# Attention and two MLPs on one core: scores on eight PE tiles, transposes of two tokens in the first two batches

## The chip, the cores and the metric

The kernel runs on one core of one Trainium2 chip. The time is the device time of one execution in microseconds (us). The core has a matrix engine (PE, with weight loads shown as PEld), a vector engine (DVE), a scalar engine (ACT), GpSimd (POOL, nearly unused here) and one queue, SP, from which this kernel issues all its transfers.

## The reference

There are 8 batches of 8 heads, 576 tokens and 64 elements a head, and 32 packed tokens `p` a head. Two attentions follow each other, and then two MLPs over all 4608 tokens (512 wide, 2048 hidden):

```python
s = scale * np.matmul(qq, kk.transpose(0, 1, 3, 2))      # sm_attn(qq, kk, vv)
a = np.exp(s - max(s)); a = a / (sum(a) + 1e-09); return np.matmul(a, vv)
...
p_packed = sm_attn(p, k, v)                # 32 x 576 scores a head
out = sm_attn(q, p_packed, p_packed)       # 576 x 32 scores a head
x = out.transpose(0, 2, 1, 3).reshape(B * S, H * D)
h = x @ w_in;  x = (h * sigmoid(h)) @ w_out
h = x @ w_in2; return (h * np.cos(h)) @ w_out2
```

## The kernel before

**Planner.** Every instruction is first recorded in a `Plan`, which then orders all engines at once: a list scheduler takes, on each engine, the ready operation that is due first, with a cost for each operation from a table (`price`) and a fixed cost for each transfer that SP issues. What stands in the code in one place can so stand elsewhere in the program. All transfers stand in one queue, SP, in the planned order: one that waits for a buffer holds those behind it.

**Stages.** The first MLP runs over four pairs of batches (`first`, with banks `hb` and `acc`); attention of the next batches runs between its matmuls. The second MLP follows (`second`) and holds no attention. In the first pair the MLP is cut into 16 runs, each of which ends with four writes of partial sums from two `ysb` buffers to DRAM (`ydram`, `ypart`).

**Attention.** `stage1(b, g)` and `stage2(b, g)` treat four heads, as `g` of 2 and two head pairs `j`; `h2` is the head in a pair. `turned` gives keys or queries with the 64 elements of a head on partitions and tokens in columns, two heads above each other (partitions 64*`h2`). For batches 0 and 1 (`Boot`), tokens come from `bx`, 96 rows of 6 tokens, and PE turns them by matmuls with the identity: 6 for a bank (`st`), 12 for a tile `bkt`, then a `copy` to SBUF on ACT or DVE, strided for queries. For batches 2 to 7 (`Steady`), four transfers fill a `kin` buffer in blocks of 32 x 32 and DVE transposes it into a `big` buffer.

**Scores.** `scores` writes two banks, one for each half `hf` of the tokens (288 columns). A bank takes four matmuls, one for each head of the four: 64 rows by 32 columns of the PE array, at row 64*`h2` and column 64*`j` + 32*`place(b, h2)`, where `place` is `(b + h2) % 2`. The four lie on four different tiles of the array; the second bank uses the same four tiles again. There are two calls for each batch and `g` (one in each stage), 32 in all: 24 in `Steady`, 8 in `Boot`. In stage 1 the stationary operand is `pbd`, filled by `place_p` (four transfers into `pin`, two DVE transposes for each batch); in stage 2 it is `ppf`, which holds each head on both partition halves.

**Products.** `products` multiplies `ppf` with the first MLP's weights on tiles of the same shape, with 512 columns: for batch 0 alone at the start (four tiles, one bank), later for two batches at once (`mb` and `sb`), whose `place` differs, so that the eight matmuls of a pass lie on eight tiles.

**Start.** Batches 0 and 1 stand before and within the first MLP steps. PE runs fillers there (`mb<-ident`), and the weights of the first MLP are decoded on ACT and DVE (tiles `wd`, `wde`, `wy`, `w1e`, `w`).

Of the kernel before, what the change touches and what calls it, by code (L numbers as in the profile page):

```python
# [12 lines left out]
F32 = mybir.dt.float32  # L13
# [66 lines left out]
class Plan:  # L80
# [4 lines left out]
    PE, DVE, ACT, POOL, DMA, NONE = "PE", "DVE", "ACT", "POOL", "DMA", "NONE"  # L85
# [72 lines left out]
    def price(self, engine, f, out, ins):  # L158

        n = math.prod(out.shape[1:])  # L160
        m = max([math.prod(x.shape[1:]) for x in ins], default=n)
        sbuf = all(not str(x.space).endswith("PSUM") for x in ins)
        strided = 44 if ins and n >= 96 and ins[0].ap[-1][0] == 2 else 110 if n >= 96 and out.ap[-1][0] > 2 else 0
        if engine == self.PE:
            if f == "transpose":
                return 3 + n / 1.2, 0

            if ins[0].dtype == F32R:
                return n / 2.4 + (18 if n == 512 else 13), 0
            rows, k = out.shape[0], ins[0].shape[0]  # L170
            if rows == 128:
                return n * 3.33 + 10, 0
            if rows == 64:
                return n * 0.82, 0
            return {64: 30 if k == 96 else 37, 288: 127, 512: 117}[n], 0
        if engine == self.DVE:
            if f == "transpose":
                return (67 if sbuf else 160) + n / 0.92, 0
            fast = sbuf and f in ("tensor_copy", "tensor_scalar", "memset") and m == n
            if f == "scalar_tensor_tensor" and sbuf and ins[0].dtype == F32:  # L180
                return 67 + n / 0.53, 0
            return 67 + max(max(m, n) / (1.92 if fast else 0.96), 60 if f == "reciprocal" else 0) + strided, 0
        if engine == self.ACT:
            return (94 if sbuf else 51) + max(m, n) / 1.2 + (190 if f == "accumulate" else 0) + (105 if f == "sin" else 0) + strided, 0
        if engine == self.POOL:
            return 149 + (1.7 if any(0 in [st for st, _ in x.ap] for x in ins) else 2.1) * n, 0
        run = min(map(self.contiguous, (out, *ins)))
        return self.ISSUE, 4 * math.prod(out.shape) / (260 if run >= 128 else 150)
# [217 lines left out]
def attention_mlps_kernel(  # L406
# [13 lines left out]
    B, H, S, D = q.shape  # L420
# [30 lines left out]
    def ring(ts):  # L451

        at = cycle(ts)
        return lambda: next(at)
# [16 lines left out]
    def tiles(pl, shape, dtype, name, n):  # L471

        ts = [pl.tile(shape, dtype, name=f"{name}{i}") for i in range(n)]
        cells.setdefault(pl, []).extend(t.tensor.name for t in ts)
        return ts


    def place(b, h2):
        return (b + h2) % 2
# [48 lines left out]
    def copy(dst, src):  # L528
        with plan.either():
            A.copy(dst, src)  # L530
            V.tensor_copy(dst, src)
# [81 lines left out]
        combine(v[1], v[1], v[2], ALU.subtract)  # L613
        put(y[1], 5)

    pins = ring(tiles(att, [P, H // 2, 32], F32, "pin", 1))
    maxes = ring(tiles(att, [P, 2], F32, "mx", 2))
    ms = ring(tiles(att, [P, 1], F32, "m", 2))
    sumss = ring(tiles(att, [P, 1], F32, "sums", 2))
# [4 lines left out]
    a2s = ring(tiles(a2p, [P, 2, S], F32R, "a2", 4))  # L624

    def place_p(b):
        t = pins()
        for h2 in range(2):
            for x in range(2):
                r = h2 * 64 + x * 32  # L630
                DMA.dma_start(t[r : r + 32], p[b, h2::2, :, 32 * x : 32 * x + 32].rearrange("j n d -> n j d"))
        for h2 in range(2):
            r, x = slice(64 * h2, 64 * h2 + 64), NP * place(b, h2)
            V.transpose(pbds[b % 2][r, :, x : x + NP], t[r].rearrange("p j d -> p (j d)"))

    def cut(t, shape):
        t = t[:, : math.prod(shape[1:])]
# [4 lines left out]

    class Steady:


        def __init__(self):
            self.kins = ring(tiles(att, [P, NB, 32], F32, "kin", 2))
# [6 lines left out]
        def turned(self, src, b, g, bank):  # L654

            ts = []
            for j in range(2):
                x = self.kins()
                for h2 in range(2):
                    for c in range(2):  # L660
                        r = h2 * 64 + c * 32
                        DMA.dma_start(
                            x[r : r + 32],
                            src[b, 4 * g + 2 * j + h2, :, 32 * c : 32 * c + 32].rearrange("(n r) d -> r n d", r=32),
                        )
                t = self.get("kt", [P, S], g, j)
                V.transpose(t, x.rearrange("p n d -> p (n d)"))
                ts.append(t)
            return ts
# [16 lines left out]

    class Boot:


        chunks = [slice(c, c + CH) for c in range(0, S, CH)]  # L690

# [21 lines left out]
        def turned(self, src, b, g, bank):  # L713
            x = self.x["k" if src is k else "q"]
            ts = []
            for j in range(2):
                t = self.get("kt", [P, S], g, j)
                hp = 2 * g + j
                for i in range(2):
                    st = bank()  # L720
                    with plan.together():
                        for c in range(3):
                            for h2 in range(2):
                                T.matmul(
                                    st[D * h2 : D * h2 + D, c * CH : (c + 1) * CH],
                                    x[:CH, 2 * hp + h2, 3 * i + c, :],
                                    ident[:CH, :CH],
                                    start=True,
                                    stop=True,
                                )  # L730
                    part = st[:, :HALF].rearrange("p (c r) -> p c r", c=3)
                    if src is k:
                        to = t.rearrange("p (c r) -> p c r", c=NCH)
                    else:
                        to = t.rearrange("p (r c) -> p c r", c=NCH)
                    copy(to[:, 3 * i : 3 * i + 3], part)
                ts.append(t)
            return ts

        def values(self, b, g):  # L740
            return lambda c, h2, j: self.x["v"][:CH, 4 * g + 2 * j + h2, c, :]

    ppf = {}
    a2 = {}

    def scores(b, keys, queries, bank):

        sts = [bank()[:, :HALF] for _ in range(2)]
        with plan.together():
            for hf, st in enumerate(sts):  # L750
                c = slice(hf * HALF, (hf + 1) * HALF)
                for j in range(2):
                    for h2 in range(2):
                        r, x = 64 * h2, 32 * place(b, h2)
                        T.matmul(
                            st[64 * j + x : 64 * j + x + 32],
                            keys[r : r + 64, j, x : x + 32],
                            queries[j][r : r + 64, c],
                            start=True,
                            stop=True,  # L760
                        )
        return sts

    def stage1(b, g, bank, mem):
# [2 lines left out]
        kt = mem.turned(k, b, g, bank)  # L767
        a1 = mem.get("a1", [P, S], g)
        mx = maxes()
        sts = scores(b, pbds[b % 2][:, 2 * g : 2 * g + 2], kt, bank)  # L770
        for hf, st in enumerate(sts):
            V.tensor_reduce(mx[:, hf : hf + 1], st, axis=AX.X, op=ALU.max)
            copy(a1[:, hf * HALF : (hf + 1) * HALF], st)
# [39 lines left out]
    def stage2(b, g, bank, mem):  # L813

        qt = mem.turned(q, b, g, bank)
        s = mem.get("s", [P, NB, 32], g)
        sf = s.rearrange("p n r -> p (n r)")
        for hf, st in enumerate(scores(b, ppf[b, g], qt, bank)):
            V.transpose(sf[:, hf * HALF : (hf + 1) * HALF], st)
        mx = mx2s()  # L820
        V.tensor_reduce(mx, s, axis=AX.X, op=ALU.max)
        combine(s, s, mx.unsqueeze(2).to_broadcast([P, NB, 32]), ALU.subtract)
        A.activation(sf, sf, AF.Exp, scale=SCALE)
        rs = rs2s()
        V.tensor_reduce(rs, s, axis=AX.X, op=ALU.add)
        V.tensor_scalar(rs, rs, 1e-9, None, op0=ALU.add)
        V.reciprocal(rs, rs)
        combine(s, s, rs.unsqueeze(2).to_broadcast([P, NB, 32]), ALU.mult)
        at = mem.get("at", [P, S], g)
        V.transpose(at, sf)  # L830
        d = a2s()
        split(d, at)
        a2[b, g] = d
# [190 lines left out]
    def output(i, t):  # L1024

        o = oring()
        if t % 2:
            V.tensor_scalar(o, acc[t], WEIGHT**-2, None, op0=ALU.mult)
        else:
            A.activation(o, acc[t], AF.Copy, scale=WEIGHT**-2)  # L1030
        p0 = order[i] * TB + t % 2 * P
        cuts = [p0] + list(range(p0 // HALF * HALF + HALF, p0 + P, HALF)) + [p0 + P]
        for a, b in zip(cuts, cuts[1:]):
            r0 = a // HALF * S + t // 2 * HALF + a % HALF
            DMA.dma_start(out[r0 : r0 + b - a, :], o[a - p0 : b - p0])

    gt, st, m5s = {}, {}, {}

# [223 lines left out]
```

## Time and profile before

| | |
|---|---|
| time, median of 3 runs | 1538.78 us (1537.59 to 1538.87) |
| the profiled execution | 1536.31 us, span 1534.6 us |
| PE busy | 1516.4 us (99%) |
| DVE busy | 1154.6 us (75%) |
| ACT busy | 786.0 us (51%) |
| mean granted TensorE clock | 0.998 of full speed |

Busy time of PE counts overlapped matmuls once, but its matmuls are pipelined: how long a block takes is read from the start of its first matmul to the start of the next block, not from the durations, which reach into the next block. A full-precision matmul here is two instructions in the trace, a transpose one.

### The profile page before, as it was taken

What the parts mean: (1) busy time and instruction counts of PE and PEld (TensorE: products, weight loads), DVE (VectorE), ACT (ScalarE), POOL (GpSimd) and SP (SyncE); (2) the same over time, 40 slices, a digit from 0 to 9 for tenths busy, and PEclk for the clock granted to TensorE, in tenths of its full rate; (3) what the DMA queues carried; (4) which work ended last, traced back from release to release, by engine and by line L of the source; (5) the groups of instructions that cost most, each with busy time, mean ns of one, the idle gap of its engine ahead of it and who ended that gap; (6) DMA issues with size and microseconds to landing.
All of it is one profiled execution on the core that took longest, in us unless ns stands there. A gap on an engine that the chain in (4) does not pass through costs nothing.

```text
span 1534.6 us, 31226 instructions
## 1 busy us (share of the span) xinstructions
PE 1516.4 (99%) x11640; PEld 1371.0 (89%) x11640; DVE 1154.6 (75%) x2413; ACT 786.0 (51%) x1678; POOL 0.7 (0%) x6
## 2 busy tenths in 40 slices
PE   9899999999999999999999999999999999999998
PEld 7689878999889998899999999999998999999997
DVE  5999567786888778784467777888878777777665
ACT  5886544555555555554354444544444445444443
POOL 0000000000000000000000000000000000000000
PEclk9999999999999999999999999999999999999999
DMA  9786474556864766541685757778665657575560
GB/s 239 230 245 194 113 158 127 170 130 167 188 205 144 183 148 190 186 156 51 209 267 177 231 175 246 245 228 252 214 214 191 214 177 230 174 230 178 184 195 35
DMA packets 304855, 287.29 MB, mean 187 GB/s; under 512 B 166464, under 2 KB 215104, under 8 KB 304704
## 3 DMA queue, kind: packets, MB, share of 16 engines
q1 hardware_dynamic: 304704, 285.30, 62.4%
q8 instruction: 92, 1.51, 0.4%
q14 instruction: 59, 0.48, 0.1%
HBM read 232.00 MB, written 53.22 MB: 186 GB/s over the span
## 4 chain that ended last, share of the span: by engine, by line
PE 90%; DMA 4%; DVE 3%; ACT 2%; issue 1%; SPq 0%; ACTq 0%; DVEq 0%
PE acc L208 50%; PE hb L208 22%; PE sb L208 9%; PE mb L208 9%; DMA bx<-in_v 1%; DVE r L208 1%; DMA kin<-in_k 0%; DMA ysb<-ypart 0%; DMA ypart<-ysb 0%; DMA w1dram<-w1e 0%; DMA wd<-in_moe_w_in 0%; ACT bkt L208 0%; SPq L208 0%; DVE w L208 0%; DVE g L208 0%
## 5 line engine op out<-in xcount | busy, mean ns | idle before, releaser
L208 PE MATMUL acc<-g,w 128*128 128x288 f32 x3072 | 472.0, 297 | 3.0 <-ACT ysb L208 1.8
L208 PEld LDWEIGHTS acc<-g,w 128*128 128x128 f32 x3072 | 425.4, 188 | 34.5 <-issue 24.3
L208 PE MATMUL acc<-w,g 128*128 128x512 f32 x1728 | 431.6, 392 | 0.0
L208 PEld LDWEIGHTS acc<-w,g 128*128 128x128 f32 x1728 | 310.9, 189 | 55.7
L208 PE MATMUL hb<-a,w 128*128 128x288 f32 x1536 | 262.3, 298 | 4.8 <-DVE a L208 2.2
L208 PEld LDWEIGHTS hb<-a,w 128*128 128x128 f32 x1536 | 221.7, 188 | 16.6 <-issue 8.7
L208 DVE TENSOR_TENSOR g<-gf,g 128x288 fp32r<-128x288 f32 x256 | 114.9, 453 | 73.0 <-PE acc L208 52.1
L208 ACT CAST g<-gf 128x288 fp32r<-128x288 f32 x238 | 102.9, 435 | 122.4 <-PE acc L208 100.7
L208 ACT ACTIVATE gf<-hb 128x288 f32<-128x288 f32 x256 | 103.5, 411 | 102.8 <-PE hb L208 88.0
L208 DVE SCALAR_TENSOR_TENSOR gf<-gf,hb 128x288 f32<-128x288 f32 x256 | 111.8, 449 | 48.3 <-ACT gf L208 46.7
L208 ACT ACTIVATE r<-r,half_pi 128x512 f32<-128x512 f32 x144 | 103.8, 722 | 35.7 <-DVE r L208 35.5
L208 ACT CAST g<-r 128x512 fp32r<-128x512 f32 x144 | 89.7, 623 | 59.3 <-DVE r L208 57.3
L208 PEld LDWEIGHTS hb<-w,w 128*128 128x128 f32 x729 | 103.8, 190 | 7.9
L208 PE MATMUL hb<-w,w 128*128 128x256 f32 x729 | 110.0, 282 | 0.0
L208 DVE TENSOR_TENSOR g<-r,g 128x512 fp32r<-128x512 f32 x144 | 98.9, 687 | 11.1 <-ACT g L208 10.7
L208 DVE SCALAR_TENSOR_TENSOR r<-n,r 128x512 f32<-128x512 int32 x144 | 99.0, 688 | 2.2
L208 ACT ACTIVATE n<-hb 128x512 int32<-128x512 f32 x72 | 43.1, 599 | 111.9 <-PE hb L208 105.6
L208 DVE TENSOR_TENSOR hb<-hb,gf 128x256 f32<-128x256 f32 x72 | 31.1, 432 | 69.9 <-PE hb L208 69.8
L208 ACT ACTIVATE n<-mb 128x512 int32<-128x512 f32 x36 | 21.5, 598 | 98.4 <-PE mb L208 98.4
L208 PE MATMUL mb<-w,w 128*128 128x256 f32 x456 | 65.6, 282 | 0.0
L208 PE MATMUL sb<-w,w 128*128 128x256 f32 x444 | 64.1, 282 | 0.0
L208 DVE TENSOR_SCALAR r<-r 128x512 f32<-128x512 f32 x144 | 60.9, 424 | 2.6
(207 smaller groups left out, 1929.4 us busy)
## 6 DMA issues: line engine op xcount, KB each, us to landing
w<-w2s SPq DMA_DIRECT2D x504, 256.0 KB, 3.6
w2s<-wd SPq DMA_DIRECT2D x28, 512.0 KB, 3.4
wd<-in_moe_w_in SPq DMA_DIRECT2D x24, 512.0 KB, 4.8
w<-w1dram SPq DMA_DIRECT2D x48, 256.0 KB, 3.1
wd<-in_moe_w_out SPq DMA_DIRECT2D x20, 512.0 KB, 4.2
ydram<-ysb SPq DMA_DIRECT2D x64, 144.0 KB, 2.5
raw<-ydram SPq DMA_DIRECT2D x72, 128.0 KB, 3.9
w2dram<-wd SPq DMA_DIRECT2D x16, 512.0 KB, 2.8
```

Source lines behind the costliest of these rows:

```text
L208: run = lambda: emit(*[real(x) for x in args], **{k: real(x) for k, x in kw.items()})
```

## The change

`scores` asks the source of its tiles where a head lies for each half (`spot`). In `Steady`, the second half of the tokens is loaded with the two heads of a pair exchanged, so the second bank uses the four tiles that the first leaves free; each `kin` buffer is filled by eight transfers of half the size in place of four. In `Boot`, one transpose turns two neighbouring tokens of a head at once (64 elements each, 128 partitions): even tokens come to partitions 0 to 63, odd ones to 64 to 127, and the bank `hf` holds even or odd tokens, with rows 64*`hf`. Both need each head of `p` on both partition halves, so `place_p` is done twice, from two `pin` buffers (8 transfers and 4 DVE transposes for a batch). The copies behind the Boot transposes write contiguous columns for keys and queries, values are picked in the new order, and the output rows of the first two batches are written with a step of 6 rows, in pieces of up to 96. The planner's cost of a score matmul goes from 127 to 65.

```diff
-            return {64: 30 if k == 96 else 37, 288: 127, 512: 117}[n], 0
+            return {64: 30 if k == 96 else 37, 288: 65, 512: 117}[n], 0
...
-    pins = ring(tiles(att, [P, H // 2, 32], F32, "pin", 1))
+    pins = ring(tiles(att, [P, H // 2, 32], F32, "pin", 2))
...
+        for side in range(2):
+            t = pins()
+            for h2 in range(2):
+                for x in range(2):
+                    r = (h2 ^ side) * 64 + x * 32
+                    DMA.dma_start(t[r : r + 32], p[b, h2::2, :, 32 * x : 32 * x + 32].rearrange("j n d -> n j d"))
+            for h2 in range(2):
+                r, x = slice(64 * (h2 ^ side), 64 * (h2 ^ side) + 64), NP * place(b, h2)
+                V.transpose(pbds[b % 2][r, :, x : x + NP], t[r].rearrange("p j d -> p (j d)"))
...
     class Steady:
+        def spot(h2, hf):
+            return 64 * (h2 ^ hf), HALF * hf
...
                     for c in range(2):
-                        r = h2 * 64 + c * 32
-                        DMA.dma_start(
-                            x[r : r + 32],
-                            src[b, 4 * g + 2 * j + h2, :, 32 * c : 32 * c + 32].rearrange("(n r) d -> r n d", r=32),
-                        )
+                        for hf in range(2):
+                            r = (h2 ^ hf) * 64 + c * 32
+                            n = slice(hf * NB // 2, (hf + 1) * NB // 2)
+                            DMA.dma_start(
+                                x[r : r + 32, n],
+                                src[b, 4 * g + 2 * j + h2, hf * HALF : (hf + 1) * HALF, 32 * c : 32 * c + 32].rearrange(
...
     class Boot:
+        def spot(h2, hf):
+            return 64 * hf, HALF * h2
...
-                for i in range(2):
+                for h2 in range(2):
                     st = bank()
                     with plan.together():
...
+                        for m in range(3):
+                            pair = x[:CH, 4 * g + 2 * j + h2, 2 * m : 2 * m + 2, :].rearrange("r c d -> r (c d)")
+                            T.transpose(st[:, m * CH : (m + 1) * CH], pair, ident[:CH, :CH])
+                    copy(t[:, h2 * HALF : (h2 + 1) * HALF], st[:, :HALF])
...
-                        r, x = 64 * h2, 32 * place(b, h2)
+                        (r, c), x = spot(h2, hf), 32 * place(b, h2)
                         T.matmul(
                             st[64 * j + x : 64 * j + x + 32],
                             keys[r : r + 64, j, x : x + 32],
-                            queries[j][r : r + 64, c],
+                            queries[j][r : r + 64, c : c + HALF],
```

The planner places all instructions anew. The score matmuls read and write the same tiles as before, so their own rows look the same; three other places show what moves.

The first place is PE's first rows, where the keys of batch 0 are turned (`bx`) and the first scores are made (`bkt`, `pbd`); of before:

```order
L208 MATMUL mb<-ident 128x128 x8
L208 MATMUL acc_88<-ident,bx_155 64x96 x6
L208 MATMUL acc_90<-ident,bx_155 64x96 x6
L208 MATMUL mb<-ident 128x128
L208 MATMUL acc_88<-ident,bx_155 64x96 x6
L208 MATMUL acc_90<-ident,bx_155 64x96 x6
L208 MATMUL mb<-ident 128x128
L208 MATMUL acc_89<-ident,bx_155 64x96 x6
L208 MATMUL acc_88<-bkt_158,pbd_106 32x288 x2
```

and of the changed kernel:

```order
L208 MATMUL mb<-ident 128x128 x8
L208 MATMUL acc_88<-ident,bx_156 128x96 x3
L208 MATMUL acc_90<-ident,bx_156 128x96 x3
L208 MATMUL mb<-ident 128x128
L208 MATMUL acc_88<-ident,bx_156 128x96 x3
L208 MATMUL acc_90<-ident,bx_156 128x96 x3
L208 MATMUL mb<-ident 128x128
L208 MATMUL acc_89<-ident,bx_156 128x96 x3
L208 MATMUL acc_91<-ident,bx_156 128x96 x3
L208 MATMUL mb<-ident 128x64
L208 MATMUL acc_88<-bkt_159,pbd_106 32x288 x2
```

Six matmuls of 64 partitions become three transposes of 128 for each bank, and the first scores move behind one more bank of transposes.

The second place is SP's first rows (keys, values and queries of batch 0 go into `bx_155` to `bx_157`, numbered one higher after the change); of before:

```order
L208 DMA bx_155<-in_k 96x2x384 x3
L208 DMA pin_119<-in_p 32x4x32 x4
L208 DMA bx_155<-in_k 96x2x384
L208 DMA bx_156<-in_v 96x2x384 x2
L208 DMA wd_108<-in_moe_w_in 128x1024
L208 DMA bx_157<-in_q 96x2x384
```

and of the changed kernel:

```order
L208 DMA bx_156<-in_k 96x2x384 x3
L208 DMA pin_119<-in_p 32x4x32 x4
L208 DMA pin_120<-in_p 32x4x32 x4
L208 DMA bx_156<-in_k 96x2x384
L208 DMA bx_157<-in_v 96x2x384 x2
L208 DMA wd_108<-in_moe_w_in 128x1024
```

Four more transfers of `p` stand ahead of the last keys and the first values.

The third place is SP in the first pair's third quarter, where the keys (`kin`) and values (`vin`) of batches 2 and 3 are loaded between the writes of partial sums (`ypart`); of before:

```order
L208 DMA ypart_83<-ysb_153 128x288
L208 DMA ypart_83<-ysb_154 128x288
L208 DMA vin_174<-in_v 128x4x64
L208 DMA kin_172<-in_k 32x18x32 x2
L208 DMA vin_174<-in_v 64x2x64 x2
L208 DMA kin_173<-in_k 32x18x32 x4
L208 DMA ypart_83<-ysb_153 128x288
```

and of the changed kernel:

```order
L208 DMA ypart_83<-ysb_154 128x288
L208 DMA ypart_83<-ysb_155 128x288
L208 DMA vin_175<-in_v 128x4x64
L208 DMA vin_175<-in_v 64x2x64 x2
L208 DMA kin_173<-in_k 32x9x32 x5
L208 DMA kin_174<-in_k 32x9x32 x8
L208 DMA ypart_83<-ysb_154 128x288
```

Between two pairs of `ypart` writes there are now up to 16 transfers, where there were 9. Over the whole program SP issues 192 more for `kin`, 32 more for `pin` and 6 more for the output.

## Rows read from the trace of the kernel before

**Rows 1.** The page: busy us, share of the span and instructions of each engine.

```profile
PE 1516.4 (99%) x11640; PEld 1371.0 (89%) x11640; DVE 1154.6 (75%) x2413; ACT 786.0 (51%) x1678; POOL 0.7 (0%) x6
```

**Rows 2.** Stretches (us): their length, busy time of each engine, PE clock, DMA share, GB/s.

```profile
10.00:20.00 10.00, 9.93 (x157) 8.57 (x153) 5.74 (x17) 6.95 (x16) 0.00 (x0) 1.00 1.06 285
...
60.00:80.00 20.00, 20.00 (x223) 15.86 (x216) 18.03 (x38) 19.13 (x40) 0.00 (x0) 1.00 0.51 163
80.00:100.00 20.00, 17.55 (x144) 15.02 (x143) 19.91 (x41) 17.74 (x40) 0.00 (x0) 1.00 0.82 236
```

**Rows 3.** PE's longest wait from 100 us to the end: us in total, times, longest.

```profile
PE acc L208 <- ACT ysb L208: 1.8, 3, 1.2
```

**Rows 4.** PE's timeline at batch 2's first scores: start us, us, what.

```profile
172.31 0.69 PE L208 MATMUL sb<-big,pbd 64*32 64x288 f32 x8
172.81 0.67 PE L208 MATMUL mb<-big,pbd 64*32 64x288 f32 x8
173.41 1.85 PE L208 MATMUL hb<-a,w 128*128 128x288 f32 x12
...
176.29 0.60 PE L208 MATMUL sb<-ident,big 128*128 128x128 f32 x4
176.65 0.51 PE L208 MATMUL acc<-g,w 128*128 128x288 f32 x2
```

**Rows 5.** One of four equal groups of PE instructions: Steady scores by bank and operand.

```profile
L208 PE MATMUL sb<-big,pbd 64*32 64x288 f32 x96 | 8.3, 415 | 0.0
```

**Rows 6.** PE's timeline at the products of batch 0 alone.

```profile
30.49 1.06 PE L208 MATMUL mb<-w1e,ppf 64*32 64x512 f32 x8
31.38 1.04 PE L208 MATMUL sb<-w1e,ppf 64*32 64x512 f32 x8
32.34 0.72 PE L208 MATMUL hb<-ident,bx 96*64 96x96 f32 x12
```

**Rows 7.** PE's timeline at the products of two batches at once.

```profile
80.69 0.63 PE L208 MATMUL mb<-w,ppf 64*32 64x512 f32 x4
80.72 0.63 PE L208 MATMUL sb<-w,ppf 64*32 64x512 f32 x4
...
81.71 2.25 PE L208 MATMUL acc<-g,w 128*128 128x288 f32 x15
```

**Rows 8.** PE's timeline where queries of batch 1 are turned.

```profile
63.87 0.72 PE L208 MATMUL mb<-ident,bx 96*64 96x96 f32 x12
64.42 0.67 PE L208 MATMUL sb<-ident,bx 96*64 96x96 f32 x12
65.01 0.40 PE L208 MATMUL hb<-a,w 128*128 128x288 f32 x1
```

**Rows 9.** ACT's timeline: a copy of Boot keys, then one of Boot queries.

```profile
35.11 0.40 ACT L208 COPY bkt<-sb 128x288 f32<-128x288 f32 x1
...
71.12 0.70 ACT L208 COPY bkt<-sb 128x288 f32<-128x288 f32 x1
```

**Rows 10.** Instructions of the tiles `pin` and `kin`: ns min/median/max, first and last start.

```profile
L208 DVE STREAM_TRANSPOSE pbd<-pin x16: 260/306/309, 6.8 to 435.1; 64x128 f32<-64x128 f32 x16
L208 SPq DMA_DIRECT2D kin<-in_k x96: 311/496/1887, 91.1 to 541.4; - x96
```

**Rows 11.** SP's timeline at the start.

```profile
2.15 1.88 SPq L208 DMA_DIRECT2D pin<-in_p  x4
```

**Rows 12.** SP's timeline, first and last of 27 rows with no gap over 0.1 us.

```profile
178.11 2.03 SPq L208 DMA_DIRECT2D kin<-in_k  x2
...
224.51 2.86 SPq L208 DMA_DIRECT2D vin<-in_v  x5
```

**Rows 13.** Two stretches near 45 us, columns as in rows 2.

```profile
40.00:41.00 1.00, 0.00 (x0) 0.00 (x0) 1.00 (x3) 0.96 (x3) 0.00 (x0) 1.00 1.07 225
...
44.00:45.00 1.00, 1.00 (x48) 1.00 (x40) 0.88 (x3) 1.00 (x3) 0.00 (x0) 0.50 1.09 250
```

More of the change, by code (lines that the diff above doesn't have):

```diff
@@ L626, in place_p @@
     def place_p(b):
[L627 to L634, printed above, removed]
+        for side in range(2):
[7 more added lines that the diff above has]
+                V.transpose(pbds[b % 2][r, :, x : x + NP], t[r].rearrange("p j d -> p (j d)"))
     def cut(t, shape):
@@ L643, in attention_mlps_kernel @@
     class Steady:
+        @staticmethod
+        def spot(h2, hf):
+            return 64 * (h2 ^ hf), HALF * hf
         def __init__(self):
@@ L660, in turned @@
                     for c in range(2):
-                        r = h2 * 64 + c * 32
-                        DMA.dma_start(
-                            x[r : r + 32],
-                            src[b, 4 * g + 2 * j + h2, :, 32 * c : 32 * c + 32].rearrange("(n r) d -> r n d", r=32),
-                        )
+                        for hf in range(2):
[4 more added lines that the diff above has]
+                                src[b, 4 * g + 2 * j + h2, hf * HALF : (hf + 1) * HALF, 32 * c : 32 * c + 32].rearrange(
+                                    "(n r) d -> r n d", r=32
+                                ),
+                            )
                 t = self.get("kt", [P, S], g, j)
@@ L687, in attention_mlps_kernel @@
     class Boot:
+        @staticmethod
+        def spot(h2, hf):
+            return 64 * hf, HALF * h2
         chunks = [slice(c, c + CH) for c in range(0, S, CH)]
@@ L717, in turned @@
                 t = self.get("kt", [P, S], g, j)
-                hp = 2 * g + j
-                for i in range(2):
+                for h2 in range(2):
                     st = bank()
                     with plan.together():
[L722 to L736, printed above, removed]
+                        for m in range(3):
+                            pair = x[:CH, 4 * g + 2 * j + h2, 2 * m : 2 * m + 2, :].rearrange("r c d -> r (c d)")
+                            T.transpose(st[:, m * CH : (m + 1) * CH], pair, ident[:CH, :CH])
+                    copy(t[:, h2 * HALF : (h2 + 1) * HALF], st[:, :HALF])
                 ts.append(t)
@@ L740, in values, with scores @@
         def values(self, b, g):
-            return lambda c, h2, j: self.x["v"][:CH, 4 * g + 2 * j + h2, c, :]
+            return lambda c, h2, j: self.x["v"][:CH, 4 * g + 2 * j + h2, 2 * (c % 3) + c // 3, :]
     ppf = {}
     a2 = {}
-    def scores(b, keys, queries, bank):
+    def scores(b, keys, queries, bank, spot):
         sts = [bank()[:, :HALF] for _ in range(2)]
@@ L750, in scores @@
             for hf, st in enumerate(sts):
-                c = slice(hf * HALF, (hf + 1) * HALF)
                 for j in range(2):
                     for h2 in range(2):
-                        r, x = 64 * h2, 32 * place(b, h2)
+                        (r, c), x = spot(h2, hf), 32 * place(b, h2)
                         T.matmul(
@@ L769, in stage1 @@
         mx = maxes()
-        sts = scores(b, pbds[b % 2][:, 2 * g : 2 * g + 2], kt, bank)
+        sts = scores(b, pbds[b % 2][:, 2 * g : 2 * g + 2], kt, bank, mem.spot)
         for hf, st in enumerate(sts):
@@ L817, in stage2 @@
         sf = s.rearrange("p n r -> p (n r)")
-        for hf, st in enumerate(scores(b, ppf[b, g], qt, bank)):
+        for hf, st in enumerate(scores(b, ppf[b, g], qt, bank, mem.spot)):
             V.transpose(sf[:, hf * HALF : (hf + 1) * HALF], st)
@@ L1031, in output @@
         p0 = order[i] * TB + t % 2 * P
-        cuts = [p0] + list(range(p0 // HALF * HALF + HALF, p0 + P, HALF)) + [p0 + P]
+        cuts = [p0] + [c for c in range(p0 + 1, p0 + P) if c % (CH if c <= S else HALF) == 0] + [p0 + P]
         for a, b in zip(cuts, cuts[1:]):
-            r0 = a // HALF * S + t // 2 * HALF + a % HALF
-            DMA.dma_start(out[r0 : r0 + b - a, :], o[a - p0 : b - p0])
+            n, m = divmod(a, HALF)
+            if n < 2:
+                r0, step = n * S + m % CH * NCH + m // CH * 2 + t // 2, NCH
+            else:
+                r0, step = n * S + t // 2 * HALF + m, 1
+            DMA.dma_start(out[r0 : r0 + (b - a - 1) * step + 1 : step, :], o[a - p0 : b - p0])
     gt, st, m5s = {}, {}, {}
```

## The prediction

> **What bounds the kernel now.** I read the page first: PE is busy for 1516.4 of 1534.6 us, DVE for 1154.6 [rows 1]. Since PE's busy time says little of its pace, I then read its waits: from 100 us to the end the longest kind is 1.8 us in three waits, for a `ysb` copy [rows 3]. From there on PE always has work, so the time is the sum of its blocks, and a microsecond taken out of them is one off the end. Last I read stretches, because the start is not like that: from 10 to 20 us the DMA share is 1.06, so the loads bound it, and from 60 to 100 us DVE works 18.03 and then 19.91 of 20 us, ACT 19.13 and 17.74, while PE stands for 2.45 us of the last 20 [rows 2]. What PE saves before 100 us counts only in part.
>
> **Scores in batches 2 to 7.** Four groups like the one in [rows 5] hold 96 instructions each, 384 in all, 16 to a call: 24 calls. A call takes 172.31 to 173.41, 1.10 us: 0.50 for the first bank, 0.60 for the second, which ends with the change to full-size matmuls [rows 4]. What eight tiles cost is seen in the products. One batch on four tiles takes 0.89 us (30.49 to 31.38) and, with that change at its end, 0.96 (31.38 to 32.34) [rows 6]. Two batches on eight tiles, in two banks that start 0.03 us apart, take 1.02 (80.69 to 81.71) [rows 7]: twice the matmuls for 0.06 us more. These have the shape of the new scores, 64 rows by 32 columns with a bank for each half, only 512 columns in place of 288. Added to one bank of scores that is 0.60 + 0.06 = 0.66 us. The other way, 512 columns on four tiles cost 0.89 where 288 cost 0.50, so 1.02 - 0.39 = 0.63. The least is 0.60, one bank alone. I take 0.64, between the two estimates: 0.46 us saved a call, 24 x 0.46 = **11.0 us**, with ends at 10.6 and 12.0. All of it lies behind 100 us, where nothing else bounds.
>
> The Trainium skill speaks against this (TensorEngine Tiling (Array Packing), Gotcha 1: PSUM Pressure): different row tiles cannot access one PSUM bank at the same time. In batches 2 to 7 each bank still takes matmuls of both row halves, so by that rule the halves would take turns and a call would stay near 1.10 us. [Rows 7] don't agree: there, too, each bank takes both row halves, and eight matmuls pass in 1.02 us. I go by the rows and keep the rule as a rival.
>
> **The first two batches.** They have 8 calls and 32 banks of transposes. In the first 39 us the loads bound, so I count nothing there. After that, four pairs of banks turn the queries of batch 1; one pair takes 63.87 to 65.01, 1.14 us [rows 8]. Transposes of this width are not in the trace; four of 128 x 128 take 0.36 us, 0.09 each [rows 4], and 96 columns cost no more, so six cost at most 0.54. That saves 0.6 a pair, 2.4 in all, and two calls of scores save 0.9. Four banks of keys of batch 1, turned between 46 and 50 us, and one call of scores save 1.7 more by the same prices (4 x 0.3 + 0.46). Together PE has 5.0 us less to do between 39 and 100 us. On the other side stands what DVE and ACT do, since they bound there: 16 copies of Boot queries cost 0.70 us strided where a contiguous one costs 0.40 [rows 9], 4.8 us less; the four more DVE transposes of `p` for these batches cost 4 x 0.31 = 1.2 us more [rows 10]. Net that is 3.6 us less on two engines, 1.8 on each. And SP issues four more transfers of `p` ahead of the values of batch 0, at 1.88/4 = 0.47 us each [rows 11], in a stretch that the loads bound: up to 1.9 us lost. So the start gives between -1.9 and 5.0 us; I take **2.0**, about what the two engines that are full there save.
>
> **Transfers and DVE later.** The `kin` loads go from 192 issues to 384, at a median of 0.50 us on SP [rows 10]. Bytes and runs stay the same, only a transfer is half as large. Twelve more DVE transposes of `p` lie behind the start, 12 x 0.31 = 3.7 us on an engine that is busy 75% [rows 1], beside PE's matmuls: hidden, and 3.7 us if they were not. The six more output transfers are 3 us of SP beside the second MLP, nothing by the same reason. But SP is not idle where batches 2 and 3 are loaded: from 178.11 to 227.37 it issues without a gap; of the issues in those 27 rows 32 are for `kin` [rows 12]. There 32 more are 16 us, and with 8 more for `p` some 20. Queued behind them are the `ypart` writes; their two `ysb` buffers come free only when a write has landed, ACT's copy waits for the buffer, and PE's next run waits for the bank that the copy empties. The rows of the order show the writes spread with up to 16 transfers between them. PE lost 1.8 us to such copies [rows 3]. The bounds are 0 (the planner moves the loads ahead) and 20 (all of it reaches PE); as PE's wait was small with a queue already full, I take **1.0** lost. What is late next, if more is lost, are the first MLP's matmuls on batches 2 and 3, whose attention ends later.
>
> **The sum.** 11.0 + 2.0 - 1.0 = 12.0 us. The profiled execution took 1536.31 us, so 1524.3 there and a span of 1522.6. The median of the runs stands 2.47 us above that execution; on the median's scale I predict **1526.8 us**, 0.8% faster. A change of less than 0.2%, 3.1 us, can't be told from none in this kernel.
>
> **The rivals.**
>
> *Eight tiles don't run at once.* If rows 64 to 127 must wait for rows 0 to 63 within a bank, a call stays at 1.10 us, and the transposes and SP leave 2.0 - 1.0: 1538.8 - 1.0 = 1537.8. Against it stands the 1.02 us of the products [rows 7]; for it, that no score block of 288 columns was seen so packed.
>
> *The clock falls longer at the start.* The granted clock was 0.50, 1.2 GHz of 2.4, at 44 to 45 us, after PE had done nothing from 40 to 41 [rows 13]. If the boot's matmuls, now half as many instructions, leave PE emptier there and ten more microseconds run at half the clock, some 5 us are lost: 12.0 - 5.0 = 7.0, 1531.8. Against it: the clock was full from 10 to 20 us, between fillers [rows 2], and the order keeps the fillers.
>
> The Trainium skill has a rule for this (TensorE: Matmul & The Clock Gate, Part 4: PE-mode transpose): transpose mode does not count as PE being busy, so turning matmuls into transposes would keep the clock low. No trace so far shows a stretch of transposes alone; by that rule the time would be the 1531.8 above.
>
> *SP holds back the partial sums.* If most of the 20 us of added issues in and around 178 to 227 us reach PE through `ysb`, the gain is gone. Of 13.0 us gained before the SP term, 13.0 + 3.1 = 16.1 must be lost to be slower by 0.2%, four fifths of the 20. All of it: 1538.8 - 13.0 + 20.0 = 1545.8. For it speaks the full queue; against it, that the same full queue has cost PE at most the 1.8 us so far [rows 3]. Half of it gives 1535.8, still faster.
>
> *The start gives all it can and SP costs nothing*: 1538.8 - 12.0 - 5.0 = 1521.8.
>
> **How the numbers follow.** The forecast, with its own bounds 1522 to 1531: 0.70, the last case included. The clock or half of the SP term, 1531 to 1536: 0.15, nearly all still faster. Eight tiles not at once: 0.07, the same. SP slower: 0.04. The remaining 0.04 is a gain below 1522 that I can't name, from the new order as a whole. So faster 0.88, same 0.07, slower 0.05, the last a little above SP's chance because a few planned waits could add to it. For 8 in 10 the range takes the forecast, the gain below, and most of the second case: 1519 to 1534.
>
> **What would show it.** Right: score blocks of batches 2 to 7 take 0.60 to 0.66 us from their first start to the next block, the two banks start within 0.05 us of each other, and PE's waits after 100 us stay under 7 us. The transposes of the boot take under 0.1 us each. Wrong: the second bank starts 0.5 us after the first, as now; PE's wait for `ysb` copies grows from 1.8 to over 5 us, with SP's row without a gap reaching past 240 us; or the granted clock stays at 0.50 beyond 50 us. The forecast would be wrong at its base if waits other than these appear behind 100 us, as the new order has other neighbours everywhere.

## The result and the profile after

The changed kernel takes 1526.95 us (median of 4 runs, 1525.84 to 1528.98), the kernel before 1538.82 beside it; the ratio is 0.9916, with an interval of 0.9895 to 0.9936. The profiled execution took 1525.84 us, 10.5 less than that of before. The forecast was 1526.8. That it came so close is in part luck: one of its three terms was right, the two others were too small and nearly cancel, and of the three orders of the same work that were run below this one is the fastest.

The page of the changed kernel, busy time of each engine, answers to [rows 1]:

```profile
PE 1501.3 (99%) x11352; PEld 1358.0 (89%) x11352; DVE 1150.8 (76%) x2424; ACT 783.4 (51%) x1683; POOL 0.7 (0%) x6
```

PE's timeline at the first scores of batch 2 (start us, us, what) answers to [rows 4]:

```profile
168.09 0.45 PE L208 MATMUL sb<-big,pbd 64*32 64x288 f32 x4
168.11 0.45 PE L208 MATMUL mb<-big,pbd 64*32 64x288 f32 x4
168.35 0.42 PE L208 MATMUL sb<-big,pbd 64*32 64x288 f32 x4
168.38 0.42 PE L208 MATMUL mb<-big,pbd 64*32 64x288 f32 x4
168.73 0.40 PE L208 MATMUL acc<-g,w 128*128 128x288 f32 x1
```

The banks start 0.02 us apart, and the call ends after 0.64 us, where it took 1.10. That is the 0.64 of the forecast. Of the 24 calls 20 look like this, within 0.1 us. The other four took 2.72, 2.94, 2.23 and 0.94 us. One of them:

```profile
203.47 0.68 PE L208 MATMUL sb<-big,pbd 64*32 64x288 f32 x4
205.56 0.43 PE L208 MATMUL sb<-big,pbd 64*32 64x288 f32 x2 [1.41 <-DVE big L208]
205.57 0.45 PE L208 MATMUL mb<-big,pbd 64*32 64x288 f32 x4
```

PE has begun the call with the first tile of keys and waits for the second, which DVE has not turned yet. DVE's timeline there and SP's say why:

```profile
204.72 0.78 DVE L208 STREAM_TRANSPOSE big<-kin 128x576 f32<-128x576 f32 x1 [1.71 <-DMA vin<-in_v]
```

```profile
193.93 8.73 SPq L208 DMA_DIRECT2D kin<-in_k  x16
202.76 3.45 SPq L208 DMA_DIRECT2D vin<-in_v  x6
```

The DVE transpose waits for a load (the view names a `vin` load that landed about then; the tile reads the last of the 16 `kin` transfers, which landed at 204.45). SP needs 8.73 us to issue these 16, 0.55 each. SP issues without a gap over 0.35 us from 173.57 to 235.54, some 62 us, where it was 49 before [rows 12].

PE's longest waits from 100 us on answer to [rows 3]:

```profile
PE sb L208 <- DVE big L208: 2.9, 3, 1.4
PE hb L208 <- DVE gf L208: 1.4, 2, 1.0
PE acc L208 <- ACT ysb L208: 1.1, 5, 0.4
```

The wait for `ysb` copies, on which I had priced SP's load, went down from 1.8 to 1.1. A new kind has come in its place, and all rows of this view together are 7.7 us, where they were 4.9.

The start went better than forecast. PE's first matmul of the MLP begins at 37.06 us, where it was 39.32; of before, then of the changed kernel:

```profile
39.32 0.53 PE L208 MATMUL hb<-a,w 128*128 128x288 f32 x2 [0.67 <-ACT a L208]
```

```profile
37.06 0.53 PE L208 MATMUL hb<-a,w 128*128 128x288 f32 x2 [1.22 <-ACT a L208]
```

A pair of Boot banks:

```profile
65.78 0.43 PE L208 MATMUL sb<-ident,bx 96*128 96x96 f32 x3
66.06 0.46 PE L208 MATMUL mb<-ident,bx 96*128 96x96 f32 x3
66.30 0.65 PE L208 MATMUL hb<-a,w 128*128 128x288 f32 x3
```

Six transposes take 0.52 us, 0.09 each, where a pair took 1.14 [rows 8]. The best mark for the start is the first `ypart` write, the end of the MLP's fifth run, which lies ahead of all scores of batches 2 to 7. It stands in the row of these transfers (times of one issue in ns, first and last start in us); of before, then of the changed kernel:

```profile
L208 SPq DMA_DIRECT2D ypart<-ysb x48: 319/376/2035, 119.2 to 255.8; - x48
```

```profile
L208 SPq DMA_DIRECT2D ypart<-ysb x48: 319/380/623, 112.9 to 250.8; - x48
```

By that mark the changed kernel is 6.3 us ahead. Of the whole 10.5, 4.2 are left for the rest of the program, though the scores alone save 24 x 0.45 = 10.8 there. So some 6.6 us are given back behind the mark. Most of it is seen in place: the four disturbed calls took 6.2 us more than four of 0.65 us. Before, one call took 0.94 us more than the others, for an ACT copy of `ppf`.

The granted clock, two stretches as in [rows 13]:

```profile
43.00:44.00 1.00, 0.59 (x3) 0.45 (x3) 1.00 (x3) 1.00 (x4) 0.00 (x0) 0.50 1.06 233
...
52.00:53.00 1.00, 1.00 (x5) 0.74 (x4) 1.00 (x2) 0.80 (x3) 0.00 (x0) 0.50 1.09 229
```

It stays at 0.50 (1.2 GHz) from 43 to 53 us, where it was back at full by 50 before, so a part of the rival of the clock came too.

### The profile page after: what moved, and what is told of

The parts are those of the page before. It is cut to its first block, busy times and chain, and to the rows that moved or that the text cites. A ratio compares the mean times of both kernels' runs of the same rounds, so it can differ in the third digit from the quotient of the medians.

```text
span 1524.1 us, 30972 instructions
## 1 busy us (share of the span) xinstructions
PE 1501.3 (99%) x11352; PEld 1358.0 (89%) x11352; DVE 1150.8 (76%) x2424; ACT 783.4 (51%) x1683; POOL 0.7 (0%) x6
## 4 chain that ended last, share of the span: by engine, by line
PE 89%; DMA 3%; DVE 2%; SPq 2%; ACT 2%; issue 1%; DVEq 0%; ACTq 0%
PE acc L208 49%; PE hb L208 22%; PE sb L208 10%; PE mb L208 8%; SPq L208 2%; DMA bx<-in_q 1%; DMA wd<-in_moe_w_in 1%; DMA ypart<-ysb 0%; DMA bx<-in_k 0%; DMA bx<-in_v 0%; DMA kin<-in_q 0%; DMA vin<-in_v 0%; DVE r L208 0%; DVE big L208 0%; DVE w L208 0%
## 5 line engine op out<-in xcount | busy, mean ns | idle before, releaser
L208 PE MATMUL hb<-a,w 128*128 128x288 f32 x1536 | 266.1, 300 | 5.6 <-DVE gf L208 3.7
L208 ACT ACTIVATE n<-hb 128x512 int32<-128x512 f32 x72 | 43.1, 598 | 112.0 <-PE hb L208 108.3
```

What stands on the lines that cost most here:

```text
L208: run = lambda: emit(*[real(x) for x in args], **{k: real(x) for k, x in kw.items()})
```

## The experiments

**Theory:** the start gave more than 6 us, and the doubled transfers of keys and queries cost nearly what eight tiles save. **Rival:** the forecast's own terms (2 from the start, 11 from the scores, 1 lost to SP), or a loss and gain that come from the new order as such. Code is shown in part; `...` marks what is left out. All times are medians; the kernel before, run beside each group, took 1539.26, 1538.42 and 1537.53 us, single executions 1533.6 to 1544.8.

**The first two batches alone** (Steady as before, its scores planned at 127):

```diff
     class Steady:
-            return 64 * (h2 ^ hf), HALF * hf
+        spot = staticmethod(FOUR)
...
-        for side in range(2):
+        for side in range(2 if b < 2 else 1):
```

`FOUR` returns `64 * h2, HALF * hf`, the four tiles of before; a `kin` buffer takes four transfers again.

> The first two batches changed alone; batches 2 to 7 keep four transfers a kin buffer and four PE tiles. Theory (the start gave 7 us, and later SP gave back 7 of the 11 us saved in the scores): 1531 to 1533 us. Rival (my forecast's own terms: the start gives 2, the scores 11): 1536 to 1538 us.

Measured 1528.20 us, ratio 0.9928 (0.9906 to 0.9951). Nearly the whole gain of the change, more than either side expected. The first `ypart` write is at 112.9 us, as in the changed kernel.

**Batches 2 to 7 alone** (Boot, its output rows and values as before, its scores planned at 127):

```diff
     class Boot:
-            return 64 * hf, HALF * h2
+        spot = staticmethod(FOUR)
...
-        for side in range(2):
+        for side in range(1 if b < 2 else 2):
```

> Batches 2 to 7 changed alone, with eight transfers a kin buffer; the first two batches as before. Theory (SP falls behind and gives back 7 of 11 us): 1534 to 1536 us, with PE waiting in the middle of a score call for the second key or query tile. Rival (the forecast's terms, 1 us lost to SP): 1528 to 1530 us.

Measured 1538.47, ratio 1.0006 (0.9987 to 1.0026): no gain at all, above both ranges, though its undisturbed score calls take 0.65 us. Four calls take 1.4 to 2.0 us, with the wait expected. Part of it is the order at the start: its first `ypart` write is at 121.7 us, 2.5 later than before, though batches 0 and 1 are as before.

**Four transfers a kin buffer, eight tiles.** Each transfer takes every second block of 32 tokens of both heads, which one access pattern reaches; the even blocks go to the upper partitions, the odd ones to the lower, and the copy out of a bank writes every second block.

```diff
-                for h2 in range(2):
+                h = 4 * g + 2 * j
+                for hf in range(2):
                     for c in range(2):
-                        for hf in range(2):
-                            r = (h2 ^ hf) * 64 + c * 32
...
+                        r = hf * 64 + c * 32
+                        blocks = src[b, h : h + 2, :, 32 * c : 32 * c + 32].rearrange("h (n t r) d -> t r (h n) d", t=2, r=32)
+                        DMA.dma_start(x[r : r + 32], blocks[hf])
...
-            return 64 * (h2 ^ hf), HALF * hf
+            return 64 * hf, HALF * h2
+        def half(t, hf):
+            return t.rearrange("p (n t r) -> p t n r", t=2, r=32)[:, hf], "p (n r) -> p n r"
```

> The changed kernel, but a kin buffer is filled by four transfers again: even blocks of 32 tokens of both heads stand on the upper half of the partitions, odd blocks on the lower, and the order is put right where a bank is copied out. Eight tiles stay. Theory (the doubled issues of SP cost some 6 us after 100 us): 1520 to 1522 us, no stalls over 1 us inside score calls. Rival (the loss comes from the new order as such, not from SP): 1526 to 1528 us.

Measured 1517.67, ratio 0.9871 (0.9838 to 0.9904): 9.3 us below the changed kernel and 2.3 below the theory's range, which rested on a cost of 6. All 24 score calls take 0.64 or 0.65 us. Here each bank takes matmuls of one row half only, where in the changed kernel it takes both.

**The kernel before with its kin transfers cut in two:**

```diff
-                        DMA.dma_start(
-                            x[r : r + 32],
...
+                        for hf in range(2):
+                            n = slice(hf * NB // 2, (hf + 1) * NB // 2)
+                            DMA.dma_start(x[r : r + 32, n],
...
```

> The kernel before with only the kin transfers cut in two, eight in place of four. Theory (SP's pace costs PE some 6 us): 1543 to 1546 us. Rival (SP's issues are hidden): 1538 to 1540 us.

Measured 1543.12, ratio 1.0022 (1.0005 to 1.0039): slower, by 3.9 us in the medians, at the lower end of the theory. How long DVE sat idle until a `kin` load landed, by queries and keys, and the sum as the view gives it (us, times), in this kernel and then in the one with four transfers and eight tiles:

```profile
  DMA kin<-in_q: 9.5, 4
  DMA kin<-in_k: 8.5, 6
...
  DVE big L208: 18.0, 10
```

```profile
  DMA kin<-in_k: 4.8, 3
...
  DVE big L208: 4.8, 3
```

DVE's idle time for `kin` loads goes with the number of transfers: 15.2 to 18.0 us in the five kernels with eight a buffer (15.2 in the changed one), 0.3 to 9.1 in the nine with four (5.4 in the kernel before).

**Each head of p loaded once, too** (on top of e3_four_kin; DVE writes both halves from one `pin`):

```diff
-        for side in range(2):
-            t = pins()
+        t = pins()
...
+        for side in range(2):
             for h2 in range(2):
-                V.transpose(pbds[b % 2][r, :, x : x + NP], t[r].rearrange("p j d -> p (j d)"))
+                r, to, x = 64 * h2, 64 * (h2 ^ side), NP * place(b, h2)
+                V.transpose(pbds[b % 2][to : to + 64, :, x : x + NP], t[r : r + 64].rearrange("p j d -> p (j d)"))
```

> The kernel of e3_four_kin, with each head of p loaded once: four transfers and one pin buffer a batch, and the DVE transposes write both partition halves from it. Theory (four transfers ahead of the first values cost up to 1.9 us in a stretch that the loads bound): 1515.5 to 1517 us. Rival (hidden): 1517 to 1519 us.

Measured 1514.83, ratio 0.9856 (0.9833 to 0.9880). It is the fastest kernel of the study, but its interval overlaps that of e3_four_kin, so the part of `p` is not settled. The first `ypart` write comes at 110.0 us, against 111.7.

**Strided copies of the boot's queries:**

```diff
-                    copy(t[:, h2 * HALF : (h2 + 1) * HALF], st[:, :HALF])
+                    if src is k:
+                        copy(t[:, h2 * HALF : (h2 + 1) * HALF], st[:, :HALF])
+                    else:
+                        to = t.rearrange("p (r c) -> p c r", c=NCH)
+                        copy(to[:, 3 * h2 : 3 * h2 + 3], st[:, :HALF].rearrange("p (c r) -> p c r", c=3))
```

> The kernel of e3_four_kin, but the copies of the first two batches' queries write with a step of six columns again, as before the change (the queries' order, and with it the output, is then wrong). Theory (ACT and DVE bound the start, so the 16 contiguous copies brought part of its gain): 1520 to 1523 us. Rival (PE's shorter transposes brought it all): 1517 to 1519 us.

Measured 1523.98, ratio 0.9914 (0.9885 to 0.9943), above both ranges. That is 6.3 us over e3_four_kin, but the first `ypart` write is at 113.0, only 1.3 later. The rest comes behind it, where no such copy stands. The new order is left as its source, which was not shown by itself.

**One-token matmuls in the boot, scores and copies as in e3_four_kin:**

```diff
-                        for m in range(3):
-                            T.transpose(st[:, m * CH : (m + 1) * CH], pair, ident[:CH, :CH])
+                        for c in range(3):
+                            for h2 in range(2):
+                                r = D * (h2 ^ hf)
+                                T.matmul(st[r : r + D, c * CH : (c + 1) * CH], x[:CH, 4 * g + 2 * j + h2, 3 * hf + c, :],
...
```

> The kernel of e3_four_kin, but the first two batches are turned by six matmuls of one token a bank, as before the change, with the heads exchanged for the second half; copies stay contiguous and the scores stay on eight tiles. Theory (the transposes of two tokens brought much of the start's gain): 1521 to 1524 us. Rival (the start's gain came from copies and scores): 1517 to 1519 us.

Measured 1524.28, ratio 0.9916 (0.9896 to 0.9936), and the first `ypart` write at 116.8, 5.1 us later than with transposes. That speaks for the transposes as the larger part of the start's gain, but it is one order of each: the three orders of the changed kernel, below, move this mark from 112.0 to 117.4. Here the granted clock stayed at 1.00 from 30 to 60 us; with transposes (e3_four_kin) it was 0.53, 0.67 and 0.94 in these three stretches of 10 us. The kernel with transposes is ahead in spite of that.

**Order.** Five kernels do the work of another in a new order. Two exchange the planner's cost of a score matmul (e10 from the kernel before, 127 to 65; e9 from the changed kernel, 65 to 127). Three get a nudge, a smaller bias of the planner between ACT and DVE (e11 on the changed kernel, e12 on e3_four_kin, e13 on the kernel before):

```diff
-            return {64: 30 if k == 96 else 37, 288: 127, 512: 117}[n], 0
+            return {64: 30 if k == 96 else 37, 288: 65, 512: 117}[n], 0
...
-FAVOUR = 300
+FAVOUR = 250
```

> The kernel before with only the planner's cost of a score matmul changed from 127 to 65: the same work in another order, planned on a cost that four tiles do not have. Theory (the gain is the work, not the order): 1538 to 1542 us. Rival (the new order itself brings the start's gain): 1531 to 1535 us.

> The changed kernel with only the planner's cost of a score matmul set back from 65 to 127: the same work in another order. If the order alone is worth some 7 us either way, as the price did to the kernel before: anywhere from 1520 to 1534 us. If the price of 65 is what fits eight tiles and the order seldom matters: 1527 to 1530 us.

> The changed kernel with another order by a small nudge (the planner's bias between ACT and DVE 250 in place of 300), the same work. Order of small weight: 1525 to 1529 us. Order worth several us: outside of it. In either case PE stalls inside some score calls for a late key or query tile, since SP's doubled issues stay.

> The kernel of e3_four_kin with the same nudge to the order. If its 9 us below the changed kernel come from SP's halved issues, it stays 6 us or more below the changed kernel with the same nudge: 1516 to 1521 us. If they were the luck of one order: 1524 to 1528 us.

> The kernel before with the same nudge to the order. Order of small weight: 1537 to 1541 us. If the order before was an unlucky one, as the 1531.5 us with the other price suggest: 1530 to 1536 us.

Measured: before with a price of 65, 1531.53 (0.9956, 0.9942 to 0.9970); the changed kernel with 127, 1534.55 (0.9975, 0.9959 to 0.9992), and with the nudge 1532.00 (0.9954, 0.9934 to 0.9974); four transfers with the nudge 1517.09 (0.9860, 0.9834 to 0.9885); before with the nudge 1536.47 (0.9990, 0.9975 to 1.0005). The kernel before moves by 6.9 us and the changed one by 7.6 with the same work in another order. In the changed kernel the clock has a part in this. Its four runs had a mean granted clock of 0.992 to 0.997, those with 127 had 0.985 to 0.993 and those with the nudge 0.986 to 0.994; among the nudged ones the run at 0.994 took 1526.54 us and the one at 0.986 took 1538.78. No run parts the order from the clock. In the kernel before the clock doesn't explain the 6.9: it was 0.996 to 0.999 with 65, and 0.994 to 1.000 in the runs beside it. So no single pair of kernels measures a few microseconds here, and the changed kernel's was the best of its three orders. Four transfers stay 14.9 us below eight under the same nudge; of the 18.1 us between their two profiled executions, 6.3 lie ahead of the first `ypart` write and 11.8 behind.

Taken over orders, the parts come apart. The first column is the start of the first `ypart` write, the mark of the start, and the second the span less that mark, both of one profiled execution of each kernel:

| kernels | first `ypart` write | rest |
|---|---|---|
| old boot: before, e2, e5, e10, e13 | 119.2 to 121.8, mean 120.4 | |
| new boot: changed, e1, e3, e9, e11, e12 | 111.1 to 117.4, mean 113.0 | |
| four tiles, four transfers: before, e1, e10, e13 | | 1411.3 to 1415.4, mean 1413.5 |
| eight tiles, eight transfers: changed, e2, e9, e11 | | 1411.2 to 1416.5, mean 1413.6 |
| eight tiles, four transfers: e3, e6, e7, e8, e12 | | 1402.4 to 1408.1, mean 1404.8 |
| four tiles, eight transfers: e5 | | 1421.7 |

Eight tiles gain 8 to 9 us, nearly what their calls save, eight transfers cost as much, and the boot gains 7.4. On four tiles the cost of eight transfers rests on e5 alone: 8.2 us by this table, 3.9 in the medians. On eight tiles it doesn't come from the clock. Behind the mark the clock fell there in e9 (0.83 in two stretches of 10 us) and in e8 (0.83 in one); without these two the kernels stand at 1411.2 to 1414.2 against 1402.4 to 1408.1. Stalls inside score calls average 5.6 us with eight transfers and 1.2 with four, half of the difference; where the other half goes was not found.

## Why the prediction was right, and where it was not

- *Scores, 11.0 us.* Right in mechanism and size: 0.46 us a call forecast from the products of two batches, 0.45 to 0.46 measured. The Trainium skill's rule that row tiles cannot access one bank at once (TensorEngine Tiling (Array Packing), Gotcha 1: PSUM Pressure) does not hold against the trace: both banks took matmuls of both row halves here, and the first four of a bank lie within 0.45 us, each 0.43 long. With one row half to a bank (e3_four_kin) a call takes the same 0.65. That rival is out.
- *The start, 2.0 us.* Too small, and outside its own bounds in the mean over orders (7.4, with 5.0 as the upper end; 6.3 in the changed kernel). One step that failed is "In the first 39 us the loads bound, so I count nothing there": the first MLP matmul came 2.3 us earlier in the changed kernel, and 2.9 in the mean over the orders of the table (36.3 against 39.2). The other is the size of what follows: I counted up to 5.0 and took 2.0, because DVE and ACT were full, and 4.0 came in this pair, 4.5 over orders. With the matmuls back, 5.1 us were gone (one order).
- *SP, 1.0 us lost.* Too small by far; the doubled transfers cost 8 to 9 us over orders. The step that failed is "ACT's copy waits for the buffer": I followed the queue to the `ysb` writes and not to its own cargo. The planner kept the writes in time; the `kin` loads themselves came late, DVE turned them late, and PE stood inside a score call, with the next matmuls behind it. My upper bound of 20 held. The sign I named for this loss was not seen: the wait for `ysb` copies fell to 1.1 us, and SP's row without a gap ended at 235.5, short of 240. What was seen is the last one, waits of another kind behind 100 us, and a sign of being right was missed: PE's waits there came to 7.7 us, not under 7.
- *The clock.* It stayed low for some 3.5 us longer, a third of the rival's ten. What that alone cost was not measured: the kernel that kept the clock differed in its matmuls too. The Trainium skill says that transpose mode does not count as PE being busy in the same way (TensorE: Matmul & The Clock Gate, Part 4: PE-mode transpose); the clocks of e3 and e8 agree with that, but PE's pauses differ between them, so they don't show it.
- *The sum.* By rows of the profiled executions: 6.3 from the start, 10.8 from the scores, some 6.6 given back. The total of 10.5 was forecast as 12.0 by terms of 2.0, 11.0 and -1.0. Of the 6.6 the four late calls hold 6.2; what the neighbours in the new order add or take can't be told within one pair. Over orders the loss goes with the transfers. The total that came out is also one of three orders: the two others took 1532.00 and 1534.55, the last outside the range of 1519 to 1534.

## What to carry to other kernels

When a change splits transfers, follow the split transfers themselves to their reader first, and only then what is queued behind them: 0.5 us an issue is a rate, and a stretch where the queue has no gap has nothing to spare. Before splitting, look for an order of the data that one access pattern reaches and put it right where the data is copied anyway: that kept the eight tiles and gave 9 us more. Where a scheduler places everything anew, run the same work in two or three orders before believing a few tenths of a per cent, and read the granted clock of each.

## What the runs showed of the hardware

- Eight full-precision matmuls of 64 rows, 32 columns and 288 moving columns on eight tiles, in two banks with both row halves in each, take 0.64 us (the changed kernel at 168.09); four on four tiles take 0.50 (the kernel before at 172.31).
- A full-precision transpose of 96 partitions by 128 columns takes 0.09 us in a row of them at the full clock (the changed kernel at 65.78).
- SP issued 16 transfers of 36 KB in 8.73 us (the changed kernel at 193.93); a transfer half as large took a median of 0.45 us to issue, against 0.50.
- DVE transposes blocks from one partition half into the other (e6_both), so data needed on both halves is loaded once.
